# Two-layer windowed attention with a one-row gated MLP: new positions for planned operations, an earlier first score block, and the last output projection in halves

## The chip, the cores and the metric

One NeuronCore of a Trainium2 chip runs the whole program in one launch. The metric is device time in microseconds (us). The engines are TensorE (PE in the profile; its weight loads are PEld), VectorE (DVE), ScalarE (ACT), GpSimd (POOL) and SyncE (SP, which issues nearly all DMAs). Each runs its own instruction list in order and waits on semaphores for the others.

## The reference

The input is a sequence of 2048 rows of 512 values. Two layers follow each other, each made of an attention block A and a block B, and each block is added to its input:

```python
def _A_ref(x, wqkv, wo):            # 32 heads of 16, window of 256
    q, k, v = ...                   # from x @ wqkv
    scores = einsum("bhqd,bhkd->bhqk", q, k) * (Dh ** -0.5)
    mask = (i - j >= 0) & (i - j < 256)
    p = softmax(where(mask, scores, -1e9))
    return einsum("bhqk,bhkd->bhqd", p, v) @ wo
def _B_ref(x, w_r, w_gate, w_up, w_down):
    r = x @ w_r
    # the one row with the largest r gets silu(x@w_gate)*(x@w_up) @ w_down * sigmoid(r); all other rows get 0
x = x + _A_ref(_layernorm(x), ...)
x = x + _B_ref(_layernorm(x), ...)  # twice, so two layers
```

## The kernel before

The sequence is cut into 16 tiles of 128 rows, so there are 32 tiles T over the two layers. Tiles go in pairs for Q and K (`qk`, L845), singly for V (`vproj`, L908). V is stored to DRAM (`vscat`) and loaded back in a layout with one block of 32 keys per partition group (`vload`). `scores` (L962) makes, for each tile and each half of the heads (sp 0 and 1), four score blocks b of 32 keys by up to 256 queries; the matmuls use the upper or the lower 64 rows of the array. Each block is one exponential on ACT (L959) into the buffer PT. `edges` makes the last 32 queries of all blocks in one. `pv` (L1025) multiplies PT by V in up to six parts, for sp 0 on all 128 rows (L1047), for sp 1 on 64-row halves (L1052); DVE then normalises (L1069, L1071). `out_proj` (L1074) transposes the result, multiplies by wo (L839; for the last two tiles L1108) and adds the residual (L1118). `mod_tile` (L1122) then does the second layer norm on the tile: `bn_stats` (L1134), `bn_aggr` (L1135), a power on POOL (L1137), the dot product for r (L1138), and the scaled output (`x4s`; L1152 for the last two tiles), which SP stores (L1193). The row for block B is chosen early from the first 10 or 11 tiles; at the end a flag (`final_flag`, L1440) tells whether a later tile would have won, and each engine reads it, so that a slower general program can follow. `keep` and `late_fill` add matmuls whose results nobody uses.

The order of the work is made before launch by a list planner (`Sched`, `schedule` L189), with assumed durations. Each operation has an index in the order in which it is made; each group of PE steps that shares a PSUM bank has an index too. For engines other than PE, the planner picks among ready operations the one with the lowest priority number, which is a base from the tile's number plus `PR[name]` plus `OSHIFT[index]` (L155). PE steps of `scores`, `edges`, `pv`, `qk`, `vproj` and `out_proj` have a fixed place instead: they are sorted by `seq`, which is a tile position from `POS` plus `USHIFT[group index]` (L157, L210). All other PE steps (transposes, the first pair's projections, gate, up and down, fills) are loose and go in where they can start early. PSUM banks are given out in this order as well.

For a group that is not of class "s", "x" or "xp" the planner makes the first step wait for everything that any step of the group needs (L195). The last two output projections are made of two steps of two matmuls each, the first on the first half of the transposed attention, the second on the second half, in one group of class "q".

Of the kernel before, what the change touches and what calls it, by code (L numbers as in the profile page):

```python
# [8 lines left out]
F32 = mybir.dt.float32  # L9
BF16 = mybir.dt.bfloat16  # L10
I32 = mybir.dt.int32
ALU = mybir.AluOpType
ACTF = mybir.ActivationFunctionType
# [483 lines left out]
PR = {"mask": 0.182, "emask": 0.827, "kprod": 0.191, "rden": -0.329, "onorm": -0.052, "resid": -0.017, "evq": -2.659, "evk": 0.381, "evv": 0.064, "bnst": 3.589, "bnst2": -0.146, "dot": -0.788, "evgu": 4.76, "cnt": 2.522, "lnorm": -0.752, "x2s": 2.155, "x4s": 0.829, "dtro": -3.805, "dtrx": 2.352, "vld": -0.586, "vst": -10.082, "ld_x2": -0.749, "st_scr": 6.464, "st_out": -2.855, "ld_mw": -3.15, "ld_x": -5.842, "evk0": -17.951, "lnd": 7.613, "evkd": -17.42, "kprod0": -28.428}  # L497
POS = {"s00": 0.135, "s01": 0.078, "s02": 0.232, "s03": 0.334, "s10": 0.484, "s11": 0.512, "s12": 0.729, "s13": 0.781, "e": 0.786, "p0": 0.872, "p0w": 0.025, "p0h": 0.019, "p1": 1.369, "p1w": 0.004, "p1h": 0.084, "v0": 0.974, "y": -0.361, "y0": -0.037, "y1": 0.007, "ln2": -1.176, "kb0": 2.729, "q": 0.257, "k": 0.565, "v": 0.218, "o": 0.714, "vst": -7.677, "vld": 0.211, "x0": 3.53, "x1": -0.896, "m0": 0.724, "m1": -3.142, "a0": -11.744, "a1": -10.763, "a2": 7.742, "a3": -6.082, "b0": -4.925, "b1": 0.094, "b2": -0.435, "b3": -8.035, "c0": -44.342, "c1": -46.015, "c2": 5.514, "d0": 0.452, "d1": -0.814, "d2": -0.508, "d3": -1.969, "e0": 0.375, "e1": -1.144, "e2": 0.087, "e3": -3.282, "ln": -2.781, "ln1": -5.211, "gu0": -5.834, "gu1": 2.222, "ac0": -0.398, "ac1": 1.79, "dn0": -3.995, "dn1": 1.247, "dw0": 3.378, "dw1": 6.885, "r2": 1.588, "z_mask": 0.18, "z_rden": -4.723, "z_onorm": -0.942, "z_resid": -9.415, "z_ag": -1.871, "z_dot": 0.365, "z_r": 0.585, "z_ev": -4.0, "z_cnt": 0.345, "oa": 0.011, "ob": -0.011, "eg0": 5.997, "eg1": -7.037, "gp0": 3.098, "gp1": 1.833, "dp0": -0.116, "dp1": -1.338, "k1": -0.171, "zp": -7.691, "zv": -2.172, "mk": 3.985, "kb": -2.575, "l1": 0.901}
USHIFT = {34: -0.098, 35: 0.029, 38: 0.005, 42: 0.081, 43: 0.293, 46: 0.012, 47: -0.133, 54: -0.014, 56: -0.069, 57: 0.026, 61: 0.014, 64: 0.061, 65: -0.055, 71: -0.051, 73: -0.111, 75: 0.003, 89: 0.07, 91: 0.002, 94: 0.202, 96: 0.071, 99: -0.249, 100: 0.022, 103: 0.033, 105: 0.083, 106: 0.033, 107: -0.022, 110: 0.08, 111: 0.03, 120: -0.042, 122: 0.049, 125: 0.027, 136: 0.016, 140: -0.001, 151: 0.022, 158: 0.024, 159: 0.015, 161: 0.044, 164: 0.033, 187: 0.038, 188: -0.009, 190: 0.006, 199: 0.016, 203: 0.026, 211: -0.006, 212: 0.063, 214: 0.125, 226: -0.12, 231: -0.018, 238: 0.052, 244: -0.019, 245: -0.031, 247: 0.008, 253: 0.038, 259: -0.027, 261: 0.01, 262: -0.014, 266: 0.114, 276: 0.005, 279: -0.148, 282: -0.018, 287: 0.027, 288: -0.137, 290: -0.024, 294: 0.041, 300: 0.04, 302: 0.018, 303: -0.107, 308: 0.139, 310: 0.029, 313: -0.072, 315: 0.001, 316: 0.045, 317: 0.019, 320: -0.081, 322: -0.045, 323: 0.116, 324: 0.099, 331: -0.116, 332: -0.119, 337: -0.059, 338: 0.039, 341: 0.043, 343: 0.04, 347: 0.051, 351: -0.192, 358: 0.094, 359: -0.036, 361: -0.058, 364: 0.009, 365: 0.035, 366: 0.159, 367: 0.009, 374: 0.006, 375: -0.045, 393: 0.023, 397: 0.174, 398: 0.005, 400: -0.023, 402: 0.084, 403: -0.031, 405: -0.018, 409: 0.005, 410: -0.082, 412: 0.1, 414: 0.068, 416: 0.053, 419: -0.028, 428: 0.051, 429: 0.048, 430: 0.009, 431: -0.004, 434: -0.021, 440: 0.034, 447: 0.018, 448: 0.022, 450: 0.092, 468: -0.015, 469: -0.282, 470: -0.009, 472: -0.057, 473: -0.065, 479: 0.024, 491: -0.027, 499: -0.015, 512: -0.002, 519: -0.108}
OSHIFT = {177: -0.096, 179: 0.626, 196: -0.205, 237: -0.199, 249: -0.154, 253: -0.116, 296: -0.043, 311: -0.576, 329: -0.016, 333: 0.047, 334: -0.006, 356: 0.808, 364: 0.98, 378: 0.008, 409: 0.067, 411: 0.408, 440: -0.268, 480: 0.043, 534: -0.541, 543: 0.056, 553: 0.064, 573: 0.047, 622: 0.305, 627: 0.105, 650: -0.49, 718: 0.765, 770: 1.211, 800: -0.129, 812: 0.787, 828: 1.374, 840: -0.084, 868: -0.319, 927: 0.207, 935: -0.207, 946: 0.004, 954: 0.121, 1022: 0.085, 1030: -0.055, 1033: 0.134, 1262: 0.343, 1285: -0.798, 1313: -0.141, 1315: -0.012, 1373: -0.37, 1376: 0.173, 1429: -0.433, 1447: -1.165, 1514: 0.634, 1521: 0.038, 1529: -0.438, 1534: -0.07, 1608: -0.666, 1617: 0.12, 1651: -0.21, 1659: 0.196, 1716: 0.02, 1718: 0.7, 1735: -0.029, 1771: -0.083, 1776: -0.246, 1783: -0.02, 1786: 0.212, 1805: 0.112, 1823: 0.058, 1851: -0.604, 1868: 0.291, 1883: 0.28, 1914: -0.559, 1928: -0.192, 1936: 0.544, 1952: 0.003, 1954: 0.352, 1970: 0.07, 1980: -0.041, 1983: 0.069, 2030: -1.316, 2033: 0.205, 2060: 0.42, 2072: -0.052, 2073: -1.962, 2083: 0.021, 2085: 1.029, 2089: 0.977, 2109: -0.31, 2131: 0.395, 2154: -0.257, 2220: -0.541, 2232: 1.251, 2240: -1.278, 2248: -0.486, 2276: 1.155, 2335: 0.813, 2344: -0.132, 2379: -0.703, 2399: 1.869, 2421: 0.104, 2422: -0.327, 2440: 0.722, 2468: -0.018, 2585: -0.33}  # L500
# [5 lines left out]
FULL, HALF = 1, 2  # L506
# [9 lines left out]
URG = 0.821  # L516
# [9 lines left out]
class Builder:  # L526
# [16 lines left out]
    def alloc(self):  # L543
# [37 lines left out]
        self.ST6M = self.sb("ST6M", [128, 2, 6], F32)  # L581
        self.DOT = self.sb("DOT", [128, 2, 2], F32)
# [491 lines left out]
    def out_proj(self, T, at):  # L1074
        S = self.S
        k2 = T % 2
# [6 lines left out]
        if last:  # L1083
            for hf in range(2):
                G = S.group("q")
# [16 lines left out]
            G = S.group("q")  # L1102
            ix = None
            for p in range(2):
                def f(e, p=p, G=G):
                    r = None
                    for j in (2 * p, 2 * p + 1):
                        r = e.matmul(self.PS[:, G.bank, 0:512], lhsT=self.OT[:, k2, j, :], rhs=self.WO[:, j, :], start=(j == 0), stop=(j == 3))  # L1108
                    return r
# [12 lines left out]
    def mod_tile(self, T, at):  # L1122
        S = self.S
        L, m = T // self.NT, T % self.NT
        km = m % 2
# [1426 lines left out]
```

## Time and profile before

| | |
|---|---|
| runs, us | 325.95, 326.41, 324.64; median 325.95 |
| the profiled execution, us | 326.61 |
| its span in the profile, us | 324.9 |
| mean granted TensorE clock in the span | 0.998 |
| busy: PE, DVE, ACT, POOL, us | 305.1, 272.4, 272.9, 143.7 |

The profile shows one execution. An engine is busy while one of its instructions runs; the idle time before an instruction is put down to what released it last. A matmul's end is modelled, and some matmul records are missing, so that PE shows small gaps where there are none. "issue" as a releaser means that the profile shows nothing that was waited for.

### The profile page before, as it was taken

What the parts mean: (1) busy time and instruction counts of PE and PEld (TensorE: products, weight loads), DVE (VectorE), ACT (ScalarE), POOL (GpSimd) and SP (SyncE); (2) the same over time, 40 slices, a digit from 0 to 9 for tenths busy, and PEclk for the clock granted to TensorE, in tenths of its full rate; (3) what the DMA queues carried; (4) which work ended last, traced back from release to release, by engine and by line L of the source; (5) the groups of instructions that cost most, each with busy time, mean ns of one, the idle gap of its engine ahead of it and who ended that gap; (6) DMA issues with size and microseconds to landing.
All of it is one profiled execution on the core that took longest, in us unless ns stands there. A gap on an engine that the chain in (4) does not pass through costs nothing.

```text
span 324.9 us, 16648 instructions
## 1 busy us (share of the span) xinstructions
PE 305.1 (94%) x7315; PEld 222.0 (68%) x7377; DVE 272.4 (84%) x728; ACT 272.9 (84%) x313; POOL 143.7 (44%) x322
## 2 busy tenths in 40 slices
PE   8978999999999999999998999999999999989995
PEld 3735677677766776777776567677677767767773
DVE  7987998999797878799877899879788687888793
ACT  8599999999889899988357999898989998999621
POOL 6280348688656170414733457351304222313441
PEclk9999999999999999999999999999999999999999
DMA  7826312627447968736694477989967546554502
GB/s 240 272 78 131 71 34 68 166 44 166 79 126 185 152 172 128 171 75 178 197 152 106 124 155 198 214 211 211 272 167 216 151 146 135 168 121 103 118 18 58
DMA packets 86546, 46.95 MB, mean 145 GB/s; under 512 B 52420, under 2 KB 80708, under 8 KB 86468
## 3 DMA queue, kind: packets, MB, share of 16 engines
q1 hardware_dynamic: 85380, 44.78, 58.3%
q8 instruction: 59, 0.97, 1.3%
q10 hardware_dynamic: 1088, 1.05, 1.0%
q14 instruction: 19, 0.16, 0.3%
HBM read 24.78 MB, written 13.43 MB: 118 GB/s over the span
## 4 chain that ended last, share of the span: by engine, by line
PE 77%; ACT 11%; DVE 4%; issue 3%; DMA 3%; SPq 0%; POOL 0%; POOLq 0%
PE PS L981 16%; PE PS L839 15%; PE PS L861 15%; PE PS L1047 14%; ACT PT L959 11%; PE PS L1052 9%; PE PS L1013 3%; DMA vd<-VN 2%; PE PS L666 2%; PE PS L1332 1%; PE PS L1408 1%; DVE KBD L931 1%; PE PS L1372 1%; DVE ON L1071 1%; DMA VBD<-vd 1%
## 5 line engine op out<-in xcount | busy, mean ns | idle before, releaser
L959 ACT ACTIVATE PT<-PS 128x1024 bf16<-128x1024 f32 (+4 forms) x284 | 257.6, 989 | 34.1 <-PE PS L981 33.1
L981 PE MATMUL PS<-QT,KBD 64*128 64x256 bf16 (+4 forms) x1024 | 82.3, 265 | 1.9 <-issue 0.9
L1137 POOL TENSOR_TENSOR XR<-XR,MHALF 128x1 f32<-128x1 f32 x32 | 18.9, 589 | 139.2 <-DVE XR L1136 133.8
L861 PE MATMUL PS<-XNT,WQKV 128*128 128x256 bf16 x480 | 62.6, 274 | 1.6 <-DVE ON L1071 0.8
L981 PEld LDWEIGHTS PS<-QT,KBD 64*128 64x128 bf16 x1024 | 35.6, 94 | 36.2 <-issue 14.2
L1047 PE MATMUL PS<-VBD,PT 128*128 128x68 bf16 x1488 | 55.2, 196 | 1.7 <-DMA VBD<-vd 1.3
L861 PEld LDWEIGHTS PS<-XNT,WQKV 128*128 128x128 bf16 x480 | 42.6, 98 | 17.5 <-issue 7.1
L1047 PEld LDWEIGHTS PS<-VBD,PT 128*128 128x128 bf16 x1488 | 50.8, 97 | 5.5 <-issue 3.9
L1052 PEld LDWEIGHTS PS<-VBD,PT 64*128 64x128 bf16 x2784 | 40.4, 93 | 3.4 <-ACT PT L959 1.6
L1052 PE MATMUL PS<-VBD,PT 64*128 64x34 bf16 x2784 | 41.6, 175 | 0.9 <-ACT PT L959 0.5
L992 DVE TENSOR_TENSOR PT<-PT,MSK 128x512 bf16<-128x512 bf16 x64 | 28.4, 444 | 7.9 <-ACT PT L959 7.6
L839 PE MATMUL PS<-WQKV,XNT 128*128 128x512 bf16 x99 | 26.4, 379 | 4.9 <-issue 2.9
L1071 DVE TENSOR_TENSOR ON<-PS,RD 128x256 bf16<-128x256 f32 x64 | 26.9, 420 | 1.5
L874 DVE CAST KTN<-PS 128x512 bf16<-128x512 f32 x30 | 20.6, 687 | 8.2 <-PE PS L861 8.2
L839 PE MATMUL PS<-WO,OT 128*128 128x512 bf16 x90 | 24.3, 379 | 3.3 <-issue 2.5
L931 DVE TENSOR_SCALAR KBD<-KTN,M 128x1024 bf16<-128x1024 bf16 x60 | 26.3, 488 | 0.4
L1069 DVE RECIPROCAL RD<-PS 128x16 f32<-128x16 f32 x64 | 16.1, 252 | 10.4 <-PE PS L1052 7.6
L1138 DVE SCALAR_TENSOR_TENSOR JUNK<-XR,WR 128x512 bf16<-128x512 f32 x32 | 23.6, 738 | 0.7
L923 DVE CAST VN<-PS 128x512 bf16<-128x512 f32 x30 | 20.6, 685 | 4.0 <-PE PS L839 3.9
L874 DVE CAST QT<-PS 128x512 bf16<-128x512 f32 x28 | 19.2, 684 | 5.0 <-PE PS L861 4.6
L1134 DVE BATCH_NORM_STATS2 ST6M<-XR 128x6 f32<-128x512 f32 x32 | 21.8, 681 | 0.0
L839 PEld LDWEIGHTS PS<-WQKV,XNT 128*128 128x128 bf16 x128 | 10.6, 97 | 13.5 <-issue 2.7
(149 smaller groups left out, 343.2 us busy)
## 6 DMA issues: line engine op xcount, KB each, us to landing
scr<-XR SPq DMA_DIRECT2D x12, 516.0 KB, 3.7
vd<-VN SPq DMA_DIRECT2D x16, 272.0 KB, 3.9
VBD<-vd SPq DMA_DIRECT2D x128, 34.0 KB, 2.8
XR<-scr SPq DMA_DIRECT2D x8, 512.0 KB, 4.6
XI<-in_B_w_down_dram SPq DMA_DIRECT2D x7, 256.0 KB, 3.2
out_dram<-OUTB SPq DMA_DIRECT2D x7, 256.0 KB, 4.2
XI<-in_A_x_dram SPq DMA_DIRECT2D x6, 256.0 KB, 7.4
MW<-in_B_w_up_dram SPq DMA_DIRECT2D x6, 256.0 KB, 5.2
```

The lines of the kernel that those rows point to most:

```text
L839: r = e.matmul(self.PS[:, G.bank, 0:n], lhsT=lhs(j), rhs=rhs(j), start=(j == 0), stop=(j == 3))
L861: r = e.matmul(self.PS[:, G.bank, 256 * u:256 * u + 256], lhsT=self.WQKV[:, j, c:c + 128], rhs=XNT[:, kb, 2 * h:2 * h + 2, j, :], start=(u ...
L874: S.add("dve", lambda e: e.tensor_copy(out=dst, in_=src[:, G.bank, :].rearrange("p (s t) -> p s t", s=2)), banks=[0], group=G, writes=keys ...
L931: S.add("dve", lambda e, h=h: e.tensor_scalar(out=self.KBD[:, k2, :, :, 32 * h:32 * h + 32].rearrange("p s b k -> p (s b) k"), in0=src, sc ...
L959: return e.activation(out=out, in_=i, func=ACTF.Exp, scale=0.25)
L981: r = e.matmul(self.PS[:, G.bank + x, W * u:W * u + n], lhsT=self.KBD[rows, k2, s, 4 * (T % 2) + b, :], rhs=self.QT[rows, s, q0:q0 + n], s ...
L992: S.add("dve", lambda e: e.tensor_tensor(out=P, in0=P, in1=m, op=ALU.mult), reads=["msk"], writes=["pt%d_%d" % ((4 * T + b) % 12, 2 * sp + ...
L1047: r = e.matmul(o, lhsT=self.PT[:, c:c + 128], rhs=self.VBD[:, v, kb % 4, :, 2 * s + a, :], start=isfirst and kb == blocks[0] and g == 0, s ...
L1052: r = e.matmul(self.PS[:, G.bank + x, 34 * g:34 * g + 34], lhsT=self.PT[rows, c:c + 128], rhs=self.VBD[rows, v, kb % 4, 2 * x:2 * x + 2, 2 ...
L1071: S.add("dve", lambda e: e.tensor_tensor(out=o, in0=acc()[:, :, :, 0:16], in1=rd.unsqueeze(3).broadcast_to([128, 2, 8, 16]), op=ALU.mult), ...
L1134: S.add("dve", lambda e: e.bn_stats(out=self.ST6M[:, km, :], in_=x), reads=[xk], writes=["st6m#%d" % km], dur=600, name="bnst2", prio=ag)
L1138: S.add("dve", lambda e: e.scalar_tensor_tensor(out=self.JUNK[:], in0=x, scalar=1.0, in1=self.WR16[:], op0=ALU.mult, op1=ALU.mult, accum_o ...
```

## The change

The numbers in `USHIFT` and `OSHIFT` are replaced: 255 entries where there were 126, and 257 where there were 100. Of them 190 and 164 are new or have another value. The two large ones, at the groups 28 and 34, belong to the block b = 0 of tile 0, for sp 0 and for sp 1.

The last tile's output projection is made of four steps in place of two: two column halves h of 256, each in a group of its own, the first of class "q", the second of class "x". The residual and `bn_stats` are made by column half, `bn_aggr` reads both statistics from `ST12`. The dot product is made behind the scale (it reads `rk`). The scaled output is made by ACT for columns 0 to 255 and by DVE for columns 256 to 511, and the store waits for both.

```diff
-PR = {"mask": 0.182, ...}
+PR = {"residh": 0.057, "bnsth": 0.015, "x4h": -2.2, "mask": 0.182, ...}
-USHIFT = {34: -0.098, 35: 0.029, 38: 0.005,
...
+USHIFT = {28: -6.678, 30: 0.192, 31: -0.1, 34: -5.984, 35: 0.122, 36: -0.19,
...
-OSHIFT = {177: -0.096, 179: 0.626,
...
+OSHIFT = {156: -1.002, 177: -0.096, 179: 0.626,
...
+        self.ST12 = self.sb("ST12", [128, 12], F32)
...
-            G = S.group("q")
-            ix = None
+            nh = 2 if T == 2 * self.NT - 1 else 1
+            n = 512 // nh
+            GH = [S.group("q" if h == 0 else "x") for h in range(nh)]
+            ix = [None] * nh
+            G = GH[0]
             for p in range(2):
...
+                for h in range(nh):
+                    def f(e, p=p, h=h, G=GH[h]):
+                        r = None
+                        for j in (2 * p, 2 * p + 1):
+                            r = e.matmul(self.PS[:, G.bank, 0:n], lhsT=self.OT[:, k2, j, :], rhs=self.WO[:, j, n * h:n * h + n], start=(j == 0), stop=(j == 3))
+                        return r
...
-        S.add("dve", lambda e: e.tensor_tensor(out=self.xf(T), in0=self.PS[:, G.bank, :], in1=x, op=ALU.add),
+        if T == 2 * self.NT - 1:
+            xf = self.xf(T)
+            for h in range(2):
+                S.add("dve", lambda e, G=GH[h], v=xf[:, 256 * h:256 * h + 256]: e.tensor_tensor(out=v, in0=self.PS[:, G.bank, 0:256], in1=v, op=ALU.add),
+                      banks=[0], group=GH[h], writes=["xh%d" % h] + ([self.xk(T)] if h == 0 else []), dur=420, name="residh", prio=at - URG + self.z(T, "resid"))
+                S.add("dve", lambda e, h=h, v=xf[:, 256 * h:256 * h + 256]: e.bn_stats(out=self.ST12[:, 6 * h:6 * h + 6], in_=v), reads=["xh%d" % h], writes=["st12_%d" % h],
+                      dur=410, name="bnsth", prio=at - URG + self.z(T, "resid") + 0.001)
...
+        end = T == 2 * self.NT - 1
+        if end:
+            S.add("dve", lambda e: e.bn_aggr(out=SC[:, 0:2], in_=self.ST12[:]), reads=["st12_0", "st12_1"], writes=[sk], dur=110, prio=ag)
...
+        if not end:
+            dot([])
...
+        elif end:
+            S.add("act", lambda e: e.activation(out=self.XN[:, km, 0:256], in_=x[:, 0:256], func=ACTF.Identity, scale=SC[:, 3:4], bias=RSM[:, km, 0:1]),
+                  reads=[sk, rk, "xh0"], writes=["xn#%d" % km], dur=580, name="x4h")
+            S.add("dve", lambda e: e.tensor_scalar(out=self.XN[:, km, 256:512], in0=x[:, 256:512], scalar1=SC[:, 3:4], scalar2=RSM[:, km, 0:1], op0=ALU.mult, op1=ALU.add),
+                  reads=[sk, rk, "xh1"], writes=["xnz"], dur=400, name="x4d", prio=ag)
...
+        if end:
+            dot(["xh0", "xh1", rk])
```

## Rows read from the trace of the kernel before

**Rows 1.** Windows view: stretches of time; columns: us, busy (xinstructions) by engine, PEclk, DMA, GB/s.

```profile
26.00:34.00 8.00, 7.05 (x138) 4.71 (x137) 7.67 (x20) 7.04 (x9) 1.58 (x3) 1.00 0.66 131
34.00:308.00 274.00, 263.48 (x6755) 195.18 (x6810) 232.95 (x610) 241.46 (x270) 123.10 (x269) 1.00 0.64 147
```

**Rows 2.** Groups by line, PE, 34 to 308 us: busy us, mean ns, idle before.

```profile
L839 PE MATMUL PS<-WO,OT 128*128 128x512 bf16 x89 | 24.1, 379 | 3.3 <-issue 2.5
L839 PE MATMUL PS<-WQKV,XNT 128*128 128x512 bf16 x85 | 22.9, 379 | 3.4 <-issue 2.9
```

**Rows 3.** Waits of PE, 34 to 308 us: total us, times, longest.

```profile
PE PS L981 <- issue: 0.9, 1, 0.9
PE PS L1052 <- ACT PT L959: 0.5, 1, 0.5
```

**Rows 4.** Chain that ended last, in order of time: start us, us, what.

```profile
14.38 6.78 DMA vd<-VN
```

**Rows 5.** Timeline of PE, 20 to 34 us: start us, us, what [idle before].

```profile
24.97 0.68 PE L1047 MATMUL PS<-VBD,PT 128*128 128x68 bf16 x16 [1.31 <-DMA VBD<-vd]
...
29.20 1.03 PE L861 MATMUL PS<-XNT,WQKV 128*128 128x256 bf16 x8 [0.68 <-DVE ON L1071]
```

**Rows 6.** Timeline, 12 to 24 us: first tile's scores begin.

```profile
12.85 0.66 ACT L885 ACTIVATE QT<-PS 128x256 bf16<-128x256 f32 x2
13.00 0.68 DVE L893 TENSOR_TENSOR KBD<-PS,M 128x512 bf16<-128x512 f32 x1
...
13.69 0.38 PE L839 MATMUL PS<-XNT,WQKV 128*128 128x256 bf16 x2
...
14.54 1.92 PE L861 MATMUL PS<-XNT,WQKV 128*128 128x256 bf16 x16 [0.47 <-ACT XNT L825]
...
16.50 0.60 ACT L872 ACTIVATE QT<-PS 128x512 bf16<-128x512 f32 x1 [1.46 <-PE PS L861]
```

**Rows 7.** Timeline of PE, 120 to 132 us: one run of score and projection steps.

```profile
128.50 0.39 PE L981 MATMUL PS<-QT,KBD 64*128 64x256 bf16 x4
128.82 1.05 PE L861 MATMUL PS<-XNT,WQKV 128*128 128x256 bf16 x8
129.80 0.39 PE L981 MATMUL PS<-QT,KBD 64*128 64x256 bf16 x4
130.03 1.38 PE L1052 MATMUL PS<-VBD,PT 64*128 64x34 bf16 x96
```

**Rows 8.** Timeline, 308 to 325 us: the end.

```profile
314.92 1.03 PE L1108 MATMUL PS<-WO,OT 128*128 128x512 bf16 x4
...
316.06 0.68 DVE L1118 TENSOR_TENSOR XR<-PS,XR 128x512 f32<-128x512 f32 x1
...
317.50 0.18 DVE L1135 BATCH_NORM_AGGREGATE XR<-ST6M 128x2 f32<-128x6 f32 x1
...
317.79 0.68 DVE L1138 SCALAR_TENSOR_TENSOR JUNK<-XR,WR 128x512 bf16<-128x512 f32 x1
317.96 0.92 POOL L1137 TENSOR_TENSOR XR<-XR,MHALF 128x1 f32<-128x1 f32 x1 [0.96 <-DVE XR L1136]
...
319.42 0.81 ACT L1152 ACTIVATE XN<-XR,RSM 128x512 bf16<-128x512 f32 x1 [2.37 <-DVE RSM L1146]
...
320.26 0.35 SPq L1193 DMA_DIRECT2D out_dram<-XN  x1
```

**Rows 9.** Lines 1137 and 489: duration ns min/median/max, first and last start.

```profile
L1137 POOL TENSOR_TENSOR XR<-XR,MHALF x32: 542/548/922, 44.7 to 318.0; 128x1 f32<-128x1 f32 x32
...
L489 SPq EVENT_SEMAPHORE  x2: 17/22/28, 322.1 to 324.4; - x2
```

**Rows 10.** Groups by form: busy us, mean ns, idle before.

```profile
L959 ACT ACTIVATE PT<-PS 128x512 bf16<-128x512 f32 x4 | 2.4, 594 | 2.2 <-PE PS L981 2.2
...
L959 ACT ACTIVATE PT<-PS 128x256 bf16<-128x256 f32 x4 | 1.5, 385 | 4.0 <-PE PS L981 4.0
...
L1071 DVE TENSOR_TENSOR ON<-PS,RD 128x256 bf16<-128x256 f32 x64 | 26.9, 420 | 1.5
```

## What I predict, and how

> **What bounds the kernel now.** I read the windows first. In the long middle stretch from 34 to 308 us TensorE (PE) is busy 263.48 of 274 us and ScalarE (ACT), which does the exponentials, 241.46 [rows 1]. PE is the bound, at the full granted clock, and 10.52 us are idle there. Most of that is no stall: the group rows for line 839 show 3.3 and 3.4 us of idle time before projection matmuls, with 89 and 85 records where the code issues four per projection [rows 2]; about one record in four is missing, and its place counts as idle. That leaves 10.52 - 6.7 = 3.8 us of true stalls. The view of waits agrees: its ten entries below the one for line 839 sum to 3.5 us, the first being 0.9 us (one wait that nothing in the profile explains) and the second 0.5 us for an exponential [rows 3]. Five of the ten, 1.6 us, wait for ACT, three, 0.7 us, for VectorE (DVE). So in the middle PE time is work, and an order that adds work there costs almost its whole price.
>
> The start is bound by something else. The chain shows the store of V lasting from 14.38 us for 6.78 us [rows 4], and its reload follows; the first probability-times-V step starts at 24.97 us after PE idled 1.31 us for that reload [rows 5]. Between 26 and 34 us PE idles 0.95 of 8 us, 0.68 of it in one wait for DVE's normalisation [rows 1, 5]. The end is one chain through several engines: last projection, residual, statistics, power on GpSimd (POOL), scale, ACT's output, store [rows 8].
>
> **Part 1, the first score blocks.** Positions 28 and 34 belong to the first score block of either half of tile 0. Sorted by the new numbers, the first goes to the very front of the placed order, ahead of the second pair's K and Q steps, and the other comes right behind the first K and the first Q step of that pair. Its inputs are there: DVE's masked keys end at 13.68 us (13.00 + 0.68), ACT's first Q copies at 13.51 us [rows 6]. PE runs the last first-pair projection at 13.69 for 0.38 us and then idles 0.47 us until 14.54 [rows 6], so a block, whose start-to-start time is 0.23 us [rows 7], fits into idle time. If an input were late, the K and Q steps would be queued behind it on PE, since PE takes its steps in order; the margin is about 0.4 us. ACT idles 1.46 us before its copy at 16.50 [rows 6], and its first exponential comes behind that copy; one exponential, 0.6 us at half the columns [rows 10] and so about 1 us at 1024, now lies in that gap. But the first V step cannot start before the reload lands, and the same eighteen steps stand ahead of it in both orders. SP's first stores and loads have no new positions, so I leave 24.97 us where it is. The gain is what follows: ACT comes out up to one exponential ahead and can take from the 0.95 us of idle time up to 34 us. I take -0.6 us, bounds -0.95 and 0 (V hides all).
>
> **Part 2, PE order in the middle.** I sorted the 910 placed PE steps by start position plus own position, before and after: 269 change place, 205 by one or two. Counted along the two sorted lists, the changes between steps on half the rows (scores, edges, second-half PV) and steps on all rows rise from 238 to 265, one of the 27 ahead of the first V step. Most come from a single score block put between two projections, or inside a PV step, where two blocks stood together. A change is not free: from a score block to a projection PE takes 128.82 - 128.50 = 0.32 us, from a score block to another half-row step 130.03 - 129.80 = 0.23 us [rows 7], so 0.09 us each. 26 of them cost 2.3 us, on the bound engine. The planner also drops about a hundred loose full-row steps (gate, up and down steps, fills) into the order, and at the place of a new alternation such a step costs nothing. I take 19 changes, 1.7 us, bounds 0.5 and 3.6 (40 changes, if loose steps break half-row runs further). What they buy: blocks come to ACT more evenly, so waits of PE on ACT go. I take -1.5 of the 1.6 us that wait for ACT, bounds -3.5 (all ten entries) and 0.
>
> The Trainium skill speaks against this part: TensorEngine Tiling (Array Packing), section Key Properties, says that changing the tiling mode drains TensorE, while going from one row tile to another does not. This case's trace agrees, with the 0.09 us above. By that rule alone the part is a plain loss; what it would make of the time is rival (b).
>
> **Part 3, positions of the other operations.** 164 numbers differ, for DVE 75, POOL 30, ACT 29, SP 29, PE 1. Most move an operation by less than one tile's position, in queues with slack: DVE 232.95 and POOL 123.10 of 274 us busy [rows 1]. A transpose or a V load that SP issues later could stall PE; the nearest price is one wait like the 0.68 us [rows 5], and a gain of the same kind is as possible. I take 0, bounds -0.5 and +0.7. Behind the split the last tile's indices move by a few places, so a few late entries hit neighbours; they lie beside PE work or behind the last store.
>
> **Part 4, the last projection in halves.** Now four 512-column matmuls run from 314.92, the residual starts at 316.06 and the aggregate at 317.50, 1.44 us later [rows 8]. The first step waits for both halves of the transposed attention, since a group of class "q" takes all its members' dependences to its first; in the change the second half's group has class "x" and can run its early matmuls sooner, and the first half is complete after four of 256 columns, half the time, some 0.4 us earlier. The residual may not use all of that, since DVE has the small operations of the chosen row's gate to run in that stretch. Two residual halves and two statistics halves follow: a 256-column DVE operation took 0.42 us [rows 10], so 1.68 us at most, and 1.36 us if half of the present 0.68 us is right. Value -0.2 us, bounds -0.5 and +0.25.
>
> The power on POOL took 0.92 us, while DVE ran the dot product beside it from 317.79 [rows 8]; over 32 such powers the median is 0.548 us [rows 9]. The dot product now waits for the scale's result, so the power stands alone: -0.37 us. ACT's output of 512 columns took 0.81 us [rows 8]. ACT's exponentials take 594 ns at 512 and 385 ns at 256 columns [rows 10], 0.21 us less; so ACT's half should take 0.60 us, DVE's about 0.42 us beside it: -0.2 us, bounds -0.4 and 0. Sum of the end: -0.2 - 0.37 - 0.2 = -0.8 us, bounds -1.2 and -0.1. Behind the output the dot product (0.68 us) is now in the chain to the flag; it is hidden by the store's landing: SP's last wait begins at 322.1 and ends at 324.4 us, for the store issued at 320.26 [rows 8, 9]. That is some 2 us of cover for a flag that comes a few tenths later.
>
> **Sum.** -0.6 + 1.7 - 1.5 + 0 - 0.8 = -1.2 us. The profiled execution took 326.61 us, of which 324.9 is its span; it becomes 325.4. It stands 0.66 us above the median of the runs, 325.95, so I predict 325.95 - 1.2 = 324.75 us.
>
> **Rivals.** (a) *Feeding ACT pays more than the turns.* The front gives 0.9, all waits for ACT and DVE go (2.3), the end gives 0.9, and loose steps absorb eleven of the 26 changes (15 remain, 1.4 us): -2.7, 323.25 us. For it: all those waits are for results that earlier blocks feed. Against: PE cannot be emptier than idle, and only 3.8 us are there to win.
> (b) *The turns decide, slower.* In the placed order of the middle 40 more changes at 0.09 us cost 3.6 us, stalls shrink by 0.5, the front and the end give 0.8 in all: +2.3, 328.25 us. For it: PE is the bound and its stalls are few. It decides from (1.63 + 0.8) / 0.09 = 27 changes that buy nothing. Against: loose steps and ACT's waits.
> (c) *V and the gate hide the edges.* The reload holds the start, so part 1 gives 0, and DVE's gate chain holds the residual, so the end gives 0.6 and middle stalls and turns cancel (+0.2): -0.4, 325.55 us.
> (d) *The change doesn't do what it says*: the first block's step waits behind a loose one and goes where it stood. Then part 1 is 0 and the time is that of (c).
>
> **Chances.** Forecast 0.36 (its own range 324.0 to 325.4), (a) 0.30, (c) with (d) 0.20, (b) 0.14. About 0.5%, 1.63 us, is what a measurement of this kernel can tell from no change. Faster by more than that, below 324.32: (a) and 0.08 of the forecast's share, 0.38. Slower, above 327.58: (b), 0.14. Between: 0.48. The range leaves out the far side of (a), 0.08, and most of (b), 0.12: 322.8 to 327.0 us.
>
> **What would show it.** Part 1: an exponential before 16 us, the first PV step still near 25 us, under 0.5 us idle from 26 to 34. Part 2: some 270 row-mode changes along PE, PE busy in the middle up by 1 to 2 us, the entries for ACT shorter. Part 4: power at 0.55 us, aggregate within 1.4 us of the residual's start, ACT's half at 0.6 us, the store 0.8 us sooner behind the last PV step. I am wrong if the first PV step moves by over 1 us, if the changes of row mode do not rise, or if the last wait of SP is for the flag.

## The result and the profile after

| | before | after |
|---|---|---|
| median, us | 326.48 (324.45 to 327.81) | 328.45 (326.65 to 329.37) |
| ratio, 95% interval | | 1.0057 (1.003 to 1.0084) |
| the profiled execution, us | 326.61 | 327.5 |
| its span, us | 324.9 | 325.4 |

The change is slower by about 1.9 us, where 1.2 us faster was forecast. The two profiled executions differ by only 0.9 us: the one of after lies 0.95 us below its median, the one of before 0.1 us above its own. So a trace against a trace tells which stage changed, and only the repeated times tell by how much.

First the start. Timeline of PE, 20 to 31 us, kernel after (its lines 582 to 1101 are one higher than in before, later ones by more):

```profile
23.69 0.68 PE L1048 MATMUL PS<-VBD,PT 128*128 128x68 bf16 x16 [0.39 <-DMA VBD<-vd]
...
28.94 1.05 PE L862 MATMUL PS<-XNT,WQKV 128*128 128x256 bf16 x8 [1.34 <-DMA XNT<-XN]
```

and of ACT in the same kernel:

```profile
14.65 1.03 ACT L960 ACTIVATE PT<-PS 128x1024 bf16<-128x1024 f32 x1
```

The first exponential runs at 14.65 us, in the gap that [rows 6] showed. The first PV step (probabilities times V, `pv`) starts 1.28 us sooner than in [rows 5]; then PE waits 1.34 us for a transpose, where before it waited 0.68 us for DVE. From 26 to 34 us PE now idles 1.55 us, where before it idled 0.95 and under 0.5 was forecast. At 51 us the two kernels' PV steps start within 0.03 us of each other: the lead is spent.

Second the middle. Windows view (columns as in [rows 1]), after:

```profile
26.00:34.00 8.00, 6.45 (x142) 4.64 (x136) 6.84 (x17) 6.33 (x8) 0.65 (x2) 1.00 0.80 122
34.00:308.00 274.00, 262.78 (x6703) 193.94 (x6759) 233.36 (x609) 241.11 (x267) 123.52 (x268) 1.00 0.63 147
```

and what PE waited for from 34 to 308 us (total us, times, longest), first the entries for ACT and DVE of before that [rows 3] does not show, then after; entries of "issue" are left out:

```profile
PE PS L981 <- ACT PT L959: 0.4, 2, 0.2
PE PS L861 <- ACT PT L959: 0.3, 2, 0.2
...
PE PS L981 <- DVE KBD L931: 0.3, 1, 0.3
PE PS L1052 <- DVE QT L874: 0.2, 1, 0.2
PE PS L1013 <- ACT PT L959: 0.2, 1, 0.2
PE PS L1221 <- ACT PT L959: 0.2, 1, 0.2
PE PS L861 <- DVE ON L1071: 0.2, 1, 0.2
```

```profile
PE PS L982 <- DVE PT L993: 0.7, 1, 0.7
...
PE PS L1358 <- DMA MW<-in_B_w_gate_dram: 0.5, 1, 0.5
PE PS L982 <- ACT PT L960: 0.4, 1, 0.4
PE PS L1053 <- ACT PT L960: 0.3, 1, 0.3
PE PS L1053 <- DVE QT L875: 0.2, 1, 0.2
PE PS L840 <- DVE PT L993: 0.2, 1, 0.2
PE PS L982 <- DVE KBD L932: 0.2, 1, 0.2
PE PS L1014 <- ACT PT L960: 0.2, 1, 0.2
PE PS L840 <- DVE MV L774: 0.2, 1, 0.2
PE PS L840 <- DVE ON L1072: 0.2, 1, 0.2
PE PS L840 <- DVE JUNK L1156: 0.2, 1, 0.2
```

Added by the engine waited for, these are, for ACT, 0.9 us where it was 1.6 [rows 3 has the first of five], for DVE 1.9 where it was 0.7, for DMA 0.5 where it was nothing. But the four DVE entries at L840, of 0.2 us each, stand before projections that show three of their four matmuls: each is the place of a missing record and no wait. In e9, a run below with the same PE order and nearly all records, they are not there. That leaves 1.1 us for DVE. The entry for DMA is not in e16, a second execution of the changed kernel. So 0.7 us of the waits for ACT went, and about as much came in for DVE and DMA: the three together are 2.5 us in after and 2.0 in e16, where before has 2.3. Changes of row mode along PE's records ("turns" from here on) rise from 252 to 280.

The last PV step, before and then after:

```profile
310.59 2.51 PE L1047 MATMUL PS<-VBD,PT 128*128 128x68 bf16 x72
```

```profile
312.01 2.52 PE L1048 MATMUL PS<-VBD,PT 128*128 128x68 bf16 x72
```

From the start of the first PV step to the end of the last, after takes 290.83 us (23.69 to 314.52) and before 288.13 (24.97 to 313.11), 2.70 more. Gaps of PE over 0.2 us in that stretch split it: DMA +1.89 (the 1.34 above and 0.55 for the gate weights), DVE and ACT -0.58, gaps with no releaser +0.32; the remaining +1.07 is work, added turns and small gaps. Two single executions differ by as much without any change there: e3, which has the order of before in this stretch, takes 290.39 us, 2.26 more than before, 1.99 of it in gaps with no releaser.

Third the end. Timeline from 314 us, after (to be read beside [rows 8]):

```profile
316.34 0.82 PE L1113 MATMUL PS<-WO,OT 128*128 128x256 bf16 x6
...
317.01 0.72 DVE L1126 TENSOR_TENSOR XR<-PS,XR 128x256 f32<-128x256 f32 x2
317.65 0.74 DVE L1128 BATCH_NORM_STATS2 ST<-XR 128x6 f32<-128x256 f32 x2
318.31 0.16 DVE L1373 TENSOR_TENSOR E<-GU,E 128x14 f32<-128x14 f32 x1
318.50 0.17 DVE L1374 TENSOR_TENSOR HT<-GU,E 128x14 bf16<-128x14 f32 x1
318.59 0.20 DVE L1149 BATCH_NORM_AGGREGATE XR<-ST 128x2 f32<-128x12 f32 x1
...
319.06 0.55 POOL L1154 TENSOR_TENSOR XR<-XR,MHALF 128x1 f32<-128x1 f32 x1 [0.64 <-DVE MT L1461]
...
320.16 0.60 ACT L1171 ACTIVATE XN<-XR,RSM 128x256 bf16<-128x256 f32 x1 [1.68 <-DVE RSM L1165]
...
320.16 0.41 DVE L1173 TENSOR_SCALAR XN<-XR,RSM 128x256 bf16<-128x256 f32 x1
321.41 0.22 DVE L1403 SCALAR_TENSOR_TENSOR ROWB<-PS,MT,GB 128x4 bf16<-128x4 f32 x1 [0.84 <-PE PS L1398]
321.55 0.68 DVE L1156 SCALAR_TENSOR_TENSOR JUNK<-XR,WR 128x512 bf16<-128x512 f32 x1
...
323.24 0.15 DVE L1477 CAST FLAG<-PS 1x1 int32<-1x1 f32 x1 [0.26 <-PE PS L1475]
...
320.78 0.35 SPq L1219 DMA_DIRECT2D out_dram<-XN  x1
321.84 0.36 SPq L1409 DMA_DIRECT2D out_dram<-ROWB  x1
```

The tile's store is issued 320.78 - 314.52 = 6.26 us behind the end of the last PV step, where before it was 320.26 - 313.11 = 7.15: 0.89 sooner, about as forecast. But DVE now makes both halves of residual and statistics ahead of the gate's last two steps (318.31 and 318.50), so the chosen row comes later, at 321.41, and its store is the last one. SP's last wait says so:

```profile
SPq L489 <- DMA out_dram<-ROWB: 0.6, 1, 0.6
```

### The profile page after: what moved, and what is told of

It reads as the page before. It is cut to its first block, busy times and chain, and to the rows that moved or that the text cites. A ratio compares the mean times of both kernels' runs of the same rounds, so it can differ in the third digit from the quotient of the medians.

```text
span 325.4 us, 16664 instructions
## 1 busy us (share of the span) xinstructions
PE 306.3 (94%) x7320; PEld 222.5 (68%) x7381; DVE 274.5 (84%) x731; ACT 273.3 (84%) x313; POOL 143.9 (44%) x322
## 3 DMA queue, kind: packets, MB, share of 16 engines
q10 hardware_dynamic: 1088, 1.05, 1.0%
## 4 chain that ended last, share of the span: by engine, by line
PE 80%; DVE 8%; DMA 3%; issue 3%; ACT 2%; POOL 2%; SPq 0%; POOLq 0%
PE PS L982 17%; PE PS L862 16%; PE PS L840 14%; PE PS L1048 13%; PE PS L1053 11%; PE PS L1014 3%; ACT PT L960 2%; DVE KBD L932 2%; DMA MW<-in_B_w_gate_dram 2%; PE PS L667 2%; DMA XNT<-XN 2%; PE PS L1358 1%; DVE KTN L875 1%; PE PS L1398 1%; POOL XN L789 1%
## 5 line engine op out<-in xcount | busy, mean ns | idle before, releaser
L960 ACT ACTIVATE PT<-PS 128x1024 bf16<-128x1024 f32 (+5 forms) x284 | 258.3, 989 | 36.7 <-PE PS L982 34.5
L982 PE MATMUL PS<-QT,KBD 64*128 64x256 bf16 (+3 forms) x1024 | 84.0, 265 | 1.6 <-DVE PT L993 0.7
L982 PEld LDWEIGHTS PS<-QT,KBD 64*128 64x128 bf16 x1024 | 34.8, 94 | 34.4 <-issue 12.9
L1048 PE MATMUL PS<-VBD,PT 128*128 128x68 bf16 x1488 | 56.6, 196 | 0.4 <-DMA VBD<-vd 0.4
L1053 PE MATMUL PS<-VBD,PT 64*128 64x34 bf16 x2784 | 43.0, 175 | 0.6 <-ACT PT L960 0.3
L1053 PEld LDWEIGHTS PS<-VBD,PT 64*128 64x128 bf16 x2784 | 41.7, 93 | 2.7 <-issue 0.6
L993 DVE TENSOR_TENSOR PT<-PT,MSK 128x512 bf16<-128x512 bf16 x64 | 29.2, 456 | 7.8 <-ACT PT L960 7.4
L840 PE MATMUL PS<-WQKV,XNT 128*128 128x512 bf16 x100 | 26.5, 379 | 4.5 <-issue 2.7
L840 PE MATMUL PS<-WO,OT 128*128 128x512 bf16 x90 | 24.7, 379 | 4.3 <-issue 3.7
L932 DVE TENSOR_SCALAR KBD<-KTN,M 128x1024 bf16<-128x1024 bf16 x60 | 27.1, 504 | 0.4
L1156 DVE SCALAR_TENSOR_TENSOR JUNK<-XR,WR 128x512 bf16<-128x512 f32 x32 | 22.5, 703 | 0.7
L777 POOL TENSOR_TENSOR RS<-RS,MHALF 128x1 f32<-128x1 f32 x19 | 11.0, 581 | 21.8 <-DVE RS L775 21.7
```

Of the source, the lines that this page charges most:

```text
L840: r = e.matmul(self.PS[:, G.bank, 0:n], lhsT=lhs(j), rhs=rhs(j), start=(j == 0), stop=(j == 3))
L932: S.add("dve", lambda e, h=h: e.tensor_scalar(out=self.KBD[:, k2, :, :, 32 * h:32 * h + 32].rearrange("p s b k -> p (s b) k"), in0=src, sc ...
L960: return e.activation(out=out, in_=i, func=ACTF.Exp, scale=0.25)
L982: r = e.matmul(self.PS[:, G.bank + x, W * u:W * u + n], lhsT=self.KBD[rows, k2, s, 4 * (T % 2) + b, :], rhs=self.QT[rows, s, q0:q0 + n], s ...
L993: S.add("dve", lambda e: e.tensor_tensor(out=P, in0=P, in1=m, op=ALU.mult), reads=["msk"], writes=["pt%d_%d" % ((4 * T + b) % 12, 2 * sp + ...
L1048: r = e.matmul(o, lhsT=self.PT[:, c:c + 128], rhs=self.VBD[:, v, kb % 4, :, 2 * s + a, :], start=isfirst and kb == blocks[0] and g == 0, s ...
```

## The experiments

Each run is set against the kernel before on the same chip. "Full clock" is the difference to before in us with the clock taken out: over the 272 executions that these ratios are made of, each us of clock time lost (one minus the mean granted clock, times the span) goes with 0.46 us of time, and that much is subtracted from each before the means are compared. The standard errors of the differences are 0.2 to 0.6 us. The changed kernel's first comparison gave 1.0057 (1.003 to 1.0084).

| run | what is changed | ratio (95%) | full clock |
|---|---|---|---|
| e2 | PE order, first blocks | 1.0022 (0.9985 to 1.006) | +1.1 |
| e15 | 13 places of the PE order, +26 turns | 1.0048 (1.0019 to 1.0076) | +1.5 |
| e14 | e2 less the 13 places, no added turn | 1.0031 (1.0005 to 1.0056) | +1.2 |
| e5 | other positions | 1.0102 (1.005 to 1.0154) | +2.0 |
| e10 | early ones | 1.0029 (1.0006 to 1.0052) | +0.4 |
| e11 | late ones | 1.007 (1.0033 to 1.0107) | +1.8 |
| e3 | halves | 0.9969 (0.9942 to 0.9997) | -0.6 |
| e4 | first blocks | 0.9987 (0.996 to 1.0015) | 0.0 |
| e12 | halves, first blocks | 0.9978 (0.9957 to 0.9999) | -1.1 |
| e6 | halves, gate steps first | 1.0004 (0.9976 to 1.0032) | +0.3 |
| e1 | halves, other positions | 1.0045 (1.0011 to 1.0079) | +0.8 |
| e9 | all but other positions | 1.0069 (1.0038 to 1.01) | +1.8 |
| e13 | all but the 13 places | 1.0099 (1.0065 to 1.0132) | +2.7 |
| e16 | all (the changed kernel) | 1.0111 (1.0062 to 1.016) | +1.8 |

**e1, the old PE order in the changed kernel.** All of `USHIFT` as before, so the first blocks too.

```diff
-USHIFT = {28: -6.678, 30: 0.192, ...
+USHIFT = {34: -0.098, 35: 0.029, ...
```

> The changed kernel with the USHIFT numbers of the kernel before (so no earlier first score block and the old order of PE steps); the halves and the new positions of the other operations stay. Theory T (the row-mode changes that the new PE order adds, 252 to 280, are paid in full on PE): the middle is as before, the last PV starts within 0.4 us of 310.6 us, and the time is within 0.3% of the kernel before. Rival W (the new positions of DVE, POOL, ACT and SP operations make PE wait): the last PV stays over 1 us late and the time stays 0.4 to 0.8% above the kernel before.

Measured 1.0045, in the range of W; its interval reaches down into that of T. Its executions lose 2.5 us of clock time, those of before 1.6, and at full clock +0.8 us is left, where e9 and e16 have +1.8. So a part of the loss stays without an added turn; how much, this run does not tell. The last PV step starts at 311.44 us, between what T and W said. That sign is no use: in e3, which has the order of before, it starts at 312.96, and 0.4 us was allowed.

**e2, the new PE order alone.**

```diff
-USHIFT = {34: -0.098, 35: 0.029, ...
+USHIFT = {28: -6.678, 30: 0.192, ...
```

> The kernel before with the USHIFT numbers of the change alone (new order of PE steps, earlier first score block); no halves, old positions for all other operations. T: some 280 row-mode changes, the last PV 0.8 to 2 us later than 310.6 us, the time 0.3 to 0.7% above the kernel before. W: the last PV at or before 310.6 us, time within 0.2% or faster. A third theory, F (the end alone loses the time, since the chosen row's store and the flag come later): last PV late or not, time within 0.3%, because the end is the old one.

Measured 1.0022 with an interval too wide to decide between T and W; +1.1 us at full clock. Its last PV step, at 311.86 us, is where T wanted it. Its trace has the wait for gate weights too, 1.05 us at 167.1.

**e3 and e4, the halves and the first blocks, each alone.** e3 has the code of the split and the old positions; e4 is before with two entries, 28 and 34:

```diff
-USHIFT = {34: -0.098, 35: 0.029, ...
+USHIFT = {34: -5.984, 35: 0.029, ..., 28: -6.678}
```

> The kernel before with the last projection, residual, statistics and output in halves alone; all position numbers as before. The PE order in the middle is the same, so T and W both expect the last PV within 0.4 us of 310.6. F expects that DVE makes the residual and statistics halves ahead of the last two steps of the chosen row's gate, that the store of that row is issued over 1.5 us later than at 318.8, lands last, and that the time is 0 to 0.3% above the kernel before. Against F: the output's store 0.8 us sooner is the end, time 0.2 to 0.3% below.

> The kernel before with only the positions 28 and 34 moved. First exponential before 16 us in any case. If the V reload holds the start: first PV step behind the landing of the reload, whose time is not this edit's doing, gain over the whole kernel 0 to 0.2%. If ACT's head start carries through: last PV 0.5 to 1 us earlier, 0.2 to 0.3% faster. If turns are paid: one more row-mode change, nothing to see.

The halves alone give 0.31%, 1.0 us. The store stands 6.26 us behind the last PV step, as in after, and the row's store comes last there as well (issued at 322.80, the tile's at 321.74), as theory F had it; but the time went down, not up. Over the profiles, the last store lands 10.95 to 11.34 us behind the end of the last PV step in the ten kernels without halves and 10.23 to 10.83 in the seven that have them as changed, 0.7 less in the mean.

The first blocks measure -0.13%, with an interval from -0.4 to +0.15%. The traces tell more: from the first PV step to the third it is 8.36 us in e4 and 8.35 in e12 (below), 8.54 in before and in e3, so they win 0.18 us. The idle time of PE from 26 to 34 us is 0.89 us in both, against 0.95 in before: ACT's head start hardly reaches it. What the blocks do not do is move the first PV step: in e6, e10, e11 and e15, which have not got them, that step starts at 23.8 us, as in after; in before and e3 it starts at 24.97 and 25.09. It goes with the landing of V, which varies from execution to execution. So the 1.28 us lead of after was not the change's.

**e5, the other positions alone.**

```diff
-OSHIFT = {177: -0.096, 179: 0.626, ...
+OSHIFT = {156: -1.002, 177: -0.096, ...
```

> The kernel before with the 257 new positions of operations off PE and nothing else; the order of PE steps and the tail stay as before. Theory W (these positions feed PE later and are the main loss of the change): the two experiments that hold them and their complements leave them with about 0.6 to 0.8%, so a ratio of 1.005 to 1.008, and in the trace idle time of PE behind DVE or DMA that the kernel before does not have. Theory T (turns of row mode and the new PE order are the loss, other positions lie in slack): a ratio of 0.998 to 1.002.

Measured 1.0102: on the old PE order these positions, which I had put at nothing, cost about as much as the whole change (1.0057 and, in e16, 1.0111). Six executions lose 4.3 us of clock time each, where before loses 1.7, so some 1.2 of the 3.1 us goes with the clock; 2.0 us is left at full clock. Its longest wait in the timeline of PE is in the gate stage:

```profile
167.09 0.54 PE L1332 MATMUL PS<-XST,MW 128*128 128x1 bf16 x16 [1.35 <-DMA MW<-in_B_w_gate_dram]
```

**e10 and e11, their early 62 and late 102 entries.**

In e10 the entries with an index below 1200 are the new ones and the others the old ones; in e11 it is the other way. e10:

```diff
-OSHIFT = {177: -0.096, 179: 0.626, ...
+OSHIFT = {156: -1.002, 177: -0.096, ...
```

> The kernel before with only the 62 changed positions of operations with an index below 1200, which come up to about 150 us; the PE order is that of before. Theory M (the loss of the other positions is the gate stage of the first layer at 155 to 167 us, where PE waited 0.49 us for a gathered row and 1.35 us for gate weights): nothing here, 0.998 to 1.002. Rival E (layer norms brought forward on POOL and transposes brought forward on SP between 40 and 80 us disturb the first tiles): 1.004 to 1.009, and the start of tile 15's PV step is at least 1 us later than in before.

> The kernel before with only the 102 changed positions of operations with an index of 1200 and more. Theory M: 1.004 to 1.010, with PE waits for the gathered row near 155 us and for gate weights near 167 us, together 1 to 2 us. Rival E: 0.998 to 1.002, without these waits.

The late ones carry most of it, as theory M said (1.007); the early ones measure 1.0029, a little above what M allowed and below what E said, and +0.4 us at full clock. The place came only in part. Timeline of PE, e11:

```profile
154.70 0.34 PE L1332 MATMUL PS<-XST,XI 128*128 128x1 bf16 x8 [0.49 <-DVE XST L1313]
...
169.08 0.45 PE L1372 MATMUL PS<-HT,MW 128*128 128x1 bf16 x8 [0.36 <-DVE HT L1348]
...
173.19 0.39 PE L981 MATMUL PS<-QT,KBD 64*128 64x256 bf16 x4 [1.32 <-ACT PT L959]
```

These are the first gate stage and the scores behind it. The wait of 0.49 us for the row that block B works on (`XST`) is there. The wait for gate weights that M named (1.35 us in e5) is not there; in its place is one for an exponential, 1.32 us, where before idled 0.85 with no releaser. The loads of gate weights land close to their use: in before the last lands at 165.18 us, issued at 159.33, and the step that uses it starts within some tenths of that.

**e6, the gate's last steps ahead of the halves.**

The edit is shown against e3; the statistics by halves get 10 more in the same way.

```diff
-... name="residh", prio=at - URG + self.z(T, "resid"))
+... name="residh", prio=at - URG + self.z(T, "resid") + 10.0)
```

> The kernel before with the split of the last projection, and the residual and statistics by halves given a later priority, so that DVE makes the gate's last two steps first. Theory G (in the changed kernel the chosen row's store is the end because these gate steps stand behind the halves on DVE): the row's store is issued at least 1 us sooner against the last PV step than with the halves alone, the end is then the tile's store or the flag, and the ratio is 0.993 to 0.997, 0.2 to 0.4% under the halves alone. Rival (the flag chain, or the landing of either store, ends at the same time anyway): a ratio of 0.996 to 0.999, as the halves alone.

Measured 1.0004. The row's store moved ahead of the tile's, as G wanted:

```profile
320.38 0.37 SPq L1409 DMA_DIRECT2D out_dram<-ROWB  x1
322.06 0.35 SPq L1219 DMA_DIRECT2D out_dram<-XN  x1
```

But the tile's store is then 322.06 - 314.83 = 7.23 us behind the last PV step, 0.97 more than with the halves alone: both chains need DVE in this stretch, and what one store wins the other loses. Theory G falls; its rival expected a slightly better time.

**e7 and e8, the price of a turn.** One matmul of 16 columns behind each of 180 PV steps, on half of the rows (e7: two turns each) or on all (e8: none).

```diff
+self.e_dummy = e.matmul(self.PS[:, G.bank, 480:496], lhsT=self.IDB[0:64, :], rhs=self.IDB[0:64, 0:16], ...)   # e8: 0:128
```

> The kernel before with one added matmul of 16 columns, of which nothing is used, at the end of each of 180 PV steps for the first half of the heads; it uses 64 rows of the array, so it adds two changes of row mode each, 360 in all. Read against the next run, which has the same dummies on 128 rows and no added change. Prediction's price of a change, 0.09 us: 28 to 36 us more PE time than the next run. Rival (a change costs a third or less once other work is queued): under 11 us more.

> As the run before, with the 180 dummies on all 128 rows, so no added change of row mode. Each costs a weight load and 16 columns: 5 to 15 us above the kernel before. The difference between the two runs over 360 is the price of one change.

363.93 against 332.47 us: 31.46 / 360 = 0.087 us per turn. First lines of the two pages, e7 and then e8:

```profile
PE 350.1 (97%) x7557; PEld 247.7 (69%) x7557; DVE 273.1 (76%) x728; ACT 274.7 (76%) x313; POOL 142.8 (40%) x322
```

```profile
PE 318.0 (96%) x7557; PEld 227.0 (69%) x7557; DVE 272.8 (83%) x728; ACT 273.4 (83%) x313; POOL 144.3 (44%) x322
```

The same number of instructions, 32.1 us more of busy PE. The prediction's 0.09 us from [rows 7] held. e8 by itself is 4.5 us above before, just under what was expected; e7 and e8 have two executions each.

**e9, the changed kernel with the old other positions.** Its PE order is the changed kernel's, step for step.

```diff
-OSHIFT = {156: -1.002, 177: -0.096, ...
+OSHIFT = {177: -0.096, 179: 0.626, ...
```

> The changed kernel with the positions of operations off PE put back to those of before; first blocks, PE order and halves stay as changed. Its PE order is the changed kernel's, step for step. Theory W (the other positions are the main loss): the time goes back by 0.5 to 1.0%, so a ratio of 0.996 to 1.001 to before. Theory T (the PE order with its 28 added turns is the loss): still 1.004 to 1.007.

Still 1.0069: theory W falls. Beside the new PE order these positions cost nothing that the intervals can show (with them 1.0057 and 1.0111, each on another chip; at full clock +1.8 us with and without); on the old one they cost about 1%. Nor are the waits of PE the loss here: from 34 to 308 us those for ACT, DVE and DMA sum to 2.0 us in e9, where before has 2.3. The positions also move waits about. In e9 there is no wait at the projection that waited 1.34 us in after:

```profile
27.75 1.05 PE L862 MATMUL PS<-XNT,WQKV 128*128 128x256 bf16 x8
```

In e16 it is there again:

```profile
29.24 1.05 PE L862 MATMUL PS<-XNT,WQKV 128*128 128x256 bf16 x8 [1.55 <-DMA XNT<-XN]
```

That transpose is issued at the same time in after and e9 (23.92 and 23.91 us) and lands at 28.90 and 27.22. It takes 3.3 us in the sixteen other profiles and about 5 in the two of the changed kernel (4.97 and 5.12), so it is the two sets of positions together that delay it. In these two alone a packet of the instruction queue q8 starts while it is under way (at 26.73 and 26.92 us; in e9 at 27.41). That this is the cause is not shown.

**e12, halves and first blocks.** Both edits of e3 and e4.

```diff
+USHIFT = {34: -5.984, 35: 0.029, ..., 28: -6.678}   # and the split
```

> The kernel before with the split last projection and the two first score blocks moved, and nothing else. If the two parts add up as measured alone: 0.9969 x 0.9987 = 0.9956, so 0.993 to 0.998. Rival (what is won ahead of the first PV step is given back by tile 3, as in the lead curves): 0.996 to 1.000, as the halves alone.

Measured 0.9978, where the two expectations overlap, so it does not tell them apart. With e3 it is the version to keep: both intervals end below 1.

**e13 to e15, the turns apart from the order.** Of the 188 changed places 13 are chosen, only because they take turns out of the list: e13 puts them back in the changed kernel, e14 in e2, e15 changes them alone.

```diff
-... 42: -0.027, ... 65: 0.251, ... 71: -0.133, ... 78: 0.129, ... 120: 0.071, ...
+... 42: 0.081, ... 65: -0.055, ... 71: -0.051, ... 120: -0.042, ...   # also 123, 131, 140, 199, 296, 355, 370, 463
```

> The changed kernel with 13 of its 188 changed places of PE steps (the two first score blocks not counted) put back to those of before, chosen only because each takes changes of row mode out of the sorted list: 253 planned changes as in the kernel before, where the changed kernel has 281; 16 of the PE steps stand elsewhere than in the changed kernel, 83 still elsewhere than in before. All else as changed. Theory T (the added turns are the loss, 28 x 0.087 = 2.4 us): 0.6 to 0.8% under the changed kernel in the same comparison, so about 0.997 to 1.000 to before. Rival W (the rest of the order, or the other positions, are the loss): as the changed kernel, 1.003 to 1.008.

> The kernel before with the new PE order less the same 13 places: the positions of operations off PE and the tail are those of before. 83 PE steps moved, no added turn. Theory T: 0.997 to 1.002. Rival W: 1.003 and more, since it holds nearly all of the new order.

> The kernel before with those 13 places alone changed to the new ones: 279 planned changes of row mode in place of 253, 16 steps moved. Theory T: 26 x 0.087 = 2.3 us, so 1.005 to 1.009. Rival W: 0.998 to 1.002, as a thirteenth of the places are changed.

Alone the 13 places cost 0.48%, 1.6 us, for 26 turns: a little below T's range, 0.06 us a turn. This is not a price of turns alone, since its trace also has two new waits for DVE, of up to 0.5 us at 57.7 and 0.4 us at 70.6. The rest of the order with the first blocks, without an added turn, costs 0.31%, 1.0 us, at the lower bound of what W said and above T's bound, with an interval that reaches both. In its trace the waits for ACT, DVE and DMA are as in before (2.4 us against 2.3, without the places of missing records), so its cost is not explained by them. Nor do the two add up: 2.6 us against the 0.7 that e2, which holds both, measured. In the changed kernel, too, putting the 13 places back saved nothing (1.0099 against 1.0111 for e16): there T failed, and W's range is exceeded too. What came in place of the turns stands in the waits of PE, 34 to 308 us, e13:

```profile
PE PS L840 <- issue: 6.9, 28, 2.6
PE PS L840 <- DMA vd<-VN: 1.7, 1, 1.7
PE PS L1053 <- ACT PT L960: 0.8, 2, 0.5
```

A store of V is now late by 1.7 us, which neither before nor after shows, and one gap without releaser lasts 2.6 us; it is one execution, and such gaps vary (see the end). That the other positions fit the PE order with these 13 places in it, and not the one without, would explain e13 and e5 alike; it is a reading, not shown.

**e16, the changed kernel beside them.**

> The changed kernel itself, on the chip of the three runs above, so that they can be set against it: 1.003 to 1.009 to before. Against the run that differed from it in the other positions alone (1.0069), theory T expects no gain and no loss of these positions in the company of the new PE order (within 0.3%).

Measured 1.0111; its interval and that of the first comparison share 1.0062 to 1.0084.

## Why the prediction failed

**The step that failed: the stalls bought (part 2).** The prediction put the added turns at +1.7 us and the stalls that the new order buys at -1.5. The price of a turn held: 0.087 us each on a stream of dummies, and 1.6 us for the 13 places with 26 of them (e15, where waits moved too). The Trainium skill, TensorEngine Tiling (Array Packing), section Key Properties, has such a change drain TensorE, and these runs agree in that each one costs time.

The stalls were not bought. In the four profiles that have the whole new order (after, e16, e2, e9) the waits of PE for ACT are 0.9 us where they were 1.6, so half of the -1.5 came. Waits for DVE and DMA took its place: for ACT, DVE and DMA together the four differ from before by -0.3 to +0.6 us, the places of missing records left out. The working asked only which waits would go. It did not ask what the steps put in their place wait for, and this was in none of the bounds: they ran from -3.5 to 0, with no loss. The order without its added turns even measured +1.0 us (e14, interval 0.2 to 1.8), and its waits do not show why. One reading is that an order set against one pattern of arrivals from DVE and SP loses its match when it is moved; no run shows it, and the cause of this part stays open.

**The other positions (part 3)** were put at 0, bounds -0.5 and +0.7. In the company of the new order that is what e9 against after says, as far as two chips can be set side by side. It is not because they lie in slack: alone they cost 3 us (1.02%), 2.0 at full clock, far outside the bounds.

**The first blocks (part 1)**: the first exponential came before 16 us as said, and V's landing, not the blocks, sets the first PV step, as said; but this landing varies by over 1 us between executions, so "I am wrong if it moves by over 1 us" was a bad test. What failed is the size: 0.18 us in the traces instead of 0.6, since the idle time from 26 to 34 us did not go.

**The halves (part 4)**: forecast -0.8, measured -1.0 alone (e3, interval -1.9 to -0.1), store 0.89 us sooner. The parts held: power 0.55, ACT's half 0.60, DVE's 0.41 us. Two readings failed. The aggregate came 1.58 us behind the residual's start, not within 1.4, because the gate's two steps fell between. And the end was not the tile's store with 2 us of cover: in after that store has landed by 322.5 us, and the row's store, pushed back by the halves on DVE, ends the program.

**The sum by the runs alone** is +1.6 (e15) +1.0 (e14, which has the first blocks in it) -1.0 (e3) = +1.6 us. The changed kernel showed 1.9 us in one comparison (1.0 to 2.7) and 3.6 in another (e16, 2.0 to 5.2). That these are near each other proves little, since the parts do not add up, as e2 and e13 show. A share may be the clock: the changed kernel lost 1.7 to 2.0 us of clock time per execution, before 1.1 to 1.7, which at 0.46 makes at most 0.4 us; that is argued, not shown.

**The rivals.** (b), slower because turns on the bound engine buy little, was the one that came: 328.25 forecast, 328.45 measured. It had the size by more turns (40) and some stalls shrunk; the runs had 28 turns, no net shrinking and an order that cost something of its own. So its direction was right, and that it came within 0.2 us is luck. Its chance, 0.14, was too low: its point of decision, 27 turns that buy nothing, was next to the 26 that had been counted, and what stood against it, besides the loose steps, was the hope on ACT's waits.

## What to carry to other kernels

When an order is moved on the bound engine, price the new neighbours of a step as well as the old: here the waits for one engine that went were replaced by waits for others, so a term "stalls bought" needs a bound on the side of loss. Positions on several queues that were set together are one change; a part of them, taken alone, can cost as much as the whole, and taken out it can save nothing. In a tail that runs through one engine, follow every chain that can end the program before a cover is counted on. And before two traces are compared, look how far two executions of kernels that are alike in that stretch lie apart.

## What the runs showed of the hardware

- A turn between matmuls on 64 rows and on 128 rows cost 0.087 us in 360 of them.
- PE stands still at a few places for 0.2 to 2.6 us with nothing waited for (often near 106, 162, 172, 228 to 235 and 248 us): from the first to the last PV step 0.9 to 4.1 us in all, differing between executions of kernels that are alike there (1.44 in before, 3.43 in e3). In e7, whose PE runs a tenth slower, there was no such gap over 0.2 us. The traces point to a cause: of the 51 gaps in the 18 profiles, 45 end 1.2 to 2.0 us behind the end of a packet on the instruction queue q8, which carries a block of 16 KB about every 5 us; of all matmuls only 15% start that far behind one. So PE seems to wait there for its next instructions. No run tested it. From the page of before (packets, MB, share of the DMA engines):

```profile
q8 instruction: 59, 0.97, 1.3%
```

- The granted clock falls to the lower level, 1.2 GHz, for a stretch of some 3.4 us at places that differ: near 156 to 163 us in nine profiles, between 235 and 305 us in four. Windows view, e10, and below it before at the same place:

```profile
152.80:156.20 3.40, 3.40 (x113) 2.96 (x110) 3.19 (x14) 1.33 (x3) 2.69 (x5) 1.00 1.09 128
156.50:159.90 3.40, 3.40 (x85) 2.22 (x85) 1.62 (x3) 0.66 (x2) 2.80 (x9) 0.51 0.97 292
```

```profile
156.50:159.90 3.40, 3.32 (x124) 2.65 (x121) 2.42 (x9) 0.66 (x2) 2.44 (x8) 1.00 0.73 227
```

In e10 PE was busy throughout the stretch ahead (152.80 to 156.20), most of its matmuls there being the one-column ones of the gate; before ran the same gate steps in order and kept its clock. In e13 and e14 the clock falls at 235.2 and 163.0 us, right behind gaps of 2.6 and 2.2 us. Over the stretch in e10 its PV steps went from 1.13 us ahead of those of before, at 152 us, to 0.40 behind at 163; at 180 they were 0.19 ahead, the kernel before standing still for 0.85 us at 172 in between.
- The tile's last store landed 4.1 us after its issue in before (320.26 to 324.40) and 1.7 us in after (320.78 to 322.50). It goes by its place: 3.5 to 4.2 us in the eleven profiles where it is the last store, 1.7 to 2.5 in the seven where the row's store is issued behind it.
